# A merged last store, a new order of the later steps and another split of block products between engines in a polysketch-attention plus FFN kernel

## The chip, the cores and the metric

The kernel runs on one core of a Trainium2 chip. The metric is device time in microseconds of one execution. A core has five engines that run side by side, each with its own queue of instructions: TensorE (PE; its weight loads are shown as PEld), VectorE (DVE), ScalarE (ACT), GpSimd (POOL) and SyncE (SP, which here issues nearly all DMA transfers; ScalarE issues a few). They meet through semaphores: an instruction waits until the one that it depends on has told that it is done.

## The reference: what is computed

Two blocks, one after the other. q, k and v come in float32, the sketches and the weights in float64 (loaded as 64-bit words and turned into float32 by integer steps); the result is float32.

```
a_x = x @ S1.T;  b_x = x @ S2.T                      # x = q or k, 4 batches, 4 heads, 1088 rows, 32 wide; 8 sketches
phi(x) = outer(a_x, b_x), 64 values a row
kv = phi(k).T @ v ;  z = sum of phi(k) over the rows
attn = (phi(q) @ kv) / (phi(q) @ z + 1e-6)            # (4, 4, 1088, 32)
x = attn as (4352, 128)                               # 4352 = 4 batches x 1088 tokens, heads side by side
out = ((x @ w1) * (x @ w2)) @ w3 @ w_out              # w1, w2: 128 x 1024, w3: 1024 x 1024, w_out: 1024 x 128
```

## The kernel before, in words

The program is not written as loops in the order of execution. `make_steps` defines some 1100 named steps, each a function that issues a few instructions, and the string `ORDER` (lines 63 to 127) lists all names in the order in which they are issued. The launcher at the end runs them one by one and chains the instructions of each engine in that order, so the order of the string is the order of every engine's queue. `POOL` (line 51) is the set of steps that go to GpSimd rather than VectorE; `on(name)` looks them up. `SLOTS` (line 28) gives, string by string, the buffer that each new tile of a kind takes: `b` the eight PSUM banks, `m` 32 SBUF buffers, and so on; one character per tile, in the order in which the steps ask for them. A tile that takes a buffer must wait until the readers of its former tile are through.

The work in stages:

- Steps `k0` to `k3` load keys and values of a batch, make phi(k) and the small matrices `kq` that stand for kv and z; steps `w0` to `w10` turn the 64-bit weight words into float32 (`w*.load`, `.c`, `.m` on ScalarE, `.j` on VectorE, `.a0`, `.a1` on POOL), and `f0` to `f7` fold w3 with w_out into `w3o`, so that the FFN's last two products are one.
- Steps `q0` to `q3` make the attention output of batches 0 and 1, half a batch each (512 tokens). `g0` to `g3` are their FFN: per chunk c of 128 of the 1024 columns `g0.0a` and `g0.0b` (products with w1 and w2, lines 1655 and 1665), `g0.0c` (copy of the first to SBUF, ScalarE, 1660), `g0.0m` (product of both, VectorE, 1671), `g0.0o` (product with w3o, line 1690).
- `q4` and `q6` are batches 2 and 3, 1024 tokens at once. Each goes through `tr`, `max`, `l2`, `l1`, `rm`, the sketch products on PE (`A0`, `C0`, `C1`, 32-row tiles that use four PSUM banks), their transposes on VectorE (`At`, `Ct`), splits (`sm`, `st`, `sh`, `sl`, `sc`), products and sums (`al`, `p01`, `p2`, `p12`, `dn`, `de`, `rc`), scaling of the outputs by powers of two (`bs`, `na`, `nb`, `nm`, `nr`, `ne`, `nn`), then `phi0`, `phi1`, their transposes `pT0`, `pT1` (VectorE), the product with kq (`x`, PE, line 1477) and four copies out of the banks, `xT0` and `xT2` on ScalarE, `xT1` and `xT3` on VectorE. `q4.ns` and `q6.ns` (POOL, lines 1444 and 1447) square the scales and spread them over the partitions, one small product and 16 small copies each; only the steps `oS` read the result. `qr` is the same chain for the last 64 tokens of each of the four batches.
- `h4` and `h6` replace the first two products of the FFN for the tokens of q4 and q6 (each of them 1024 tokens, the g4/g5 and g6/g7 of the third product). The products with w1 and w2 are done by blocks, with seven block products in place of eight (`prod`, line 1602): names such as `h4.1b6` are batch part h4, column block 1 (of 4), side b, product 6. Side a (w1) uses rows 0 to 63 of the array, side b (w2) rows 64 to 127. Products 1, 6, 7 and 4 add up in one PSUM tile X, 5 and 3 in Y, 2 stands alone in Z; between them ScalarE copies the sum so far to SBUF (`take`, line 1609: c, d, e, i) and VectorE adds a PSUM tile to such a copy (`plus`, line 1614: f, g, h). The sums of moving data that products 3, 5, 6 and 7 need are `h4.s1` to `h4.s4`; those of the weights are `v.1` to `v.4` (POOL). The elementwise product of sides a and b is `h4.1m11`, `m12`, `m22` (line 1636, VectorE or POOL by the set) and `m21` (line 1641, VectorE). The third product is then `g4.0o` to `g7.7o` (line 1690).
- A result leaves by `oT` (transpose out of PSUM, VectorE, line 1697), for g4 to g7 `oS` (product with the scales, line 1703), and `st`: four DMAs of 64 KB issued by SP (`main_dst`, line 1506).
- `gr` is the FFN of the 256 tokens of qr: `gr.0a`, `gr.0b`, `gr.0c`, `gr.0m` with 256 columns, and `gr.0o0`, `gr.0o1` for the two halves of 128 tokens (line 1679). `gr.oT0` (ScalarE) and `gr.oT1` (VectorE) copy the halves out of PSUM (line 1714); `gr.st0` is issued by ScalarE and `gr.st1` by SP, 64 KB each (`rest_dst`, line 1512).

Before the third product of g4 to g7 PE goes through the h4 and h6 products in four stretches: 18 products up to `qr.x`, 38 up to the g5 products, 14 between the g5 and the g4 products, 42 up to the first `gr` product.

At 34 us, in a part of the order that the diff leaves alone, PE runs `g0.6b`, `g0.0a`, `k1.T0`, `k1.T1`, and ScalarE `k2.max` (reads the keys of batch 2 as they land), `g0.7c`, `g0.4c`, `k1.Gc`, `g0.0c`.

The functions that the diff touches, and what calls them:

Of the kernel before, what the change touches and what calls it, by code (L numbers as in the profile page):

```python
# [43 lines left out]

# [4 lines left out]
QUARTERS = (0, 2, 1, 3)  # L49

POOL = set("""
    g5.oS g7.oS h4.0m12 h4.0m22 h4.1m11 h4.1m12 h4.1m22 h4.2m12 h4.2m22 h4.s4 h6.0m11 h6.0m12 h6.1m11
    h6.1m12 h6.1m22 h6.2m22 h6.3m11 h6.3m22 h6.s2 h6.s3 k0.Nh k0.Nr k0.rest0 k1.Nr k1.kp0 k1.kp1
    k1.rest0 k2.Nr k2.rest0 k3.kp0 k3.kp1 k3.rest0 q0.al q0.p01 q0.sca q1.al q1.p12 q1.phi q2.bs q2.p01
    q2.p2 q2.phi0 q2.sc q3.al q3.bs q3.p12 q3.p2 q3.phi0 q4.al q4.bs q4.nn q4.p12 q4.phi0 q4.phi1 q4.sc
    q6.al q6.p01 q6.p12 q6.p2 q6.phi1 q6.sc q6.sl qr.al qr.bs qr.p12 qr.p2 qr.phi0 qr.sl s.AR s.KS s.Pp
    s.blkh s.low
""".split())

# [31 lines left out]
g2.4b g2.2b g2.6b k3.Ta g2.3b k3.Tb k3.Tc q4.l1 g2.7m g2.4m q3.phi0 q3.pT0 w3.c kr1.kp g2.0m g2.3m g2.6m g2.2m w2.a1  # L91
w2.a0 q3.x w6.a0 f4.m w3.j f6.t w3.a1 q3.xT0 g3.4a w8.c f4.o g3.4c g3.1a q4.rm q4.A0 k3.ab q4.C0 q4.C1 k3.N0 k3.N1
k3.abt g3.3b g3.7b w3.a0 q4.At q4.Ct g3.6a f6.m g3.7a g3.0a q4.sm f0.t w4.c f6.o w6.a1 k2.kp1 f3.t g3.1c g3.6c k3.kp1
g3.0c f0.m g3.4b f3.m f3.o k3.kp0 k2.kp0 k2.kv0 k2.kv3 k2.kv1 k2.kv2 w4.j k2.kvr k2.kvc q4.st q4.sh q4.sl q4.sc k3.kv0
k3.kv1 w10.load q4.al k3.kv3 k3.kv2 k3.kvr w4.m g3.7c k3.Na f0.o k3.Nb w8.m g3.4m q4.p01 q4.p2 q4.p12 g3.0b g3.6b
w5.a0 g3.6m q4.dn g3.0m g3.2b q4.de g3.2a g2.0o v.s w8.j q4.rc g3.7m v.t w8.a1 w4.a1 g3.2c w8.a0 g2.4o k3.kvc w10.c
w10.m g3.0o g2.6o g3.3a g3.3c g3.4o f2.t q4.na w4.a0 q6.tr q6.max g3.1b g3.3m f5.t g3.1m f2.m k3.Nr q6.l2 q6.l1 f5.m
f5.o f2.o g3.5a f1.t q4.bs g3.5c q6.rm q6.A0 q6.C0 q6.C1 g2.5o q4.nb q4.nm q4.nr q4.ne q6.Ct q6.At k2.kqt g3.3o f1.m
g3.5b q6.sm q4.nn q4.phi0 q4.phi1 g3.2m q4.pT0 w10.j w10.a0 q4.pT1 g1.0o w10.a1 g3.5m q6.st q6.sh f7.t qr.rm k2.kq
# [33 lines left out]
def make_steps(ctx, tc, q, k, v, S1, S2, moe_w1, moe_w2, moe_w3, moe_w_out, out):  # L133
# [11 lines left out]
    NT = S // 32  # L145
# [1362 lines left out]
                             oT[i * 32:(i + 1) * 32, :nT * 32].rearrange("p (T d) -> p T d", d=32))  # L1508
        return dst

    def rest_dst(oT, u):
        (sp if u else act).dma_start(bass.AP(tensor=out.tensor, offset=(NT - 2 + u) * DM,
                             ap=[[NT * DM, 32], [S * DM, B], [1, DM]]), oT)
# [129 lines left out]
    def ffn(g, n, dst, halves=1):  # L1643
# [38 lines left out]
        if g != "r":  # L1682
            first = {}
            turn = [c for i in range(4) for c in (i, i + 4)] if whole else range(NC)
            for c in range(NC):
                @step(f"g{g}.{c}o")
                def _(c=c):
                    if c == turn[0]:
                        o_ps[g] = ps("out", [128, 512], "ps_o")
                    pe.matmul(o_ps[g], w3o[:, c], ab_sb[g, c], start=c == turn[0], stop=c == turn[-1])  # L1690

            oT = {}

            @step(f"g{g}.oT")
            def _():
                oT[0] = sb("oT", [128, 512], bufs=2)
                dve.transpose(oT[0], o_ps[g])

            if whole:
                @step(f"g{g}.oS")  # L1700
                def _():
                    y = oT[0].rearrange("p (t d) -> p t d", d=32)
                    on(f"g{g}.oS").tensor_mul(y, y, bview(scale[g], [[1, 16], [0, 32]]))

            step(f"g{g}.st")(lambda: dst(oT[0]))
        else:
            z = {}
            for u in range(2):
                @step(f"g{g}.oT{u}")
                def _(u=u):  # L1710
                    if u == 0:
                        z["o"] = sb("oT", [128, 512], bufs=2)
                    z[u] = z["o"][:, u * DM:(u + 1) * DM]
                    (dve.tensor_copy if u else act.copy)(z[u], o_ps[g, u])
# [76 lines left out]
```

## Time and profile before

| | |
|---|---|
| runs | 254.11, 254.26 and 259.58 us; median 254.26 |
| the profiled execution | 253.4 us, of which 251.3 us lie between its first and last instruction (the span) |
| granted TensorE clock, mean | 0.996 |
| PE busy, first to last quarter of the first 100 us | 23.78, 23.85, 24.99 and 25.00 of 25 us each |
| DMA | 22.06 MB, 88 GB/s over the span |

All times of a trace are counted from the start of the span; an execution takes some 2 us more than its span. A row of the timeline gives start, duration, engine, line, operation, what it writes and reads, how many instructions are merged in it, and in brackets how long the engine had been idle before and what ended that. A `q` behind an engine's name (SPq) means its sequencer, which waits or issues DMAs. The views of waits say who waited for what: total, number, longest.

Most of PE's float32 matmuls are recorded as two passes of one instruction each. The end of a matmul is modelled, so its starts tell more than its busy time.

### The profile page before, as it was taken

What the parts mean: (1) busy time and instruction counts of PE and PEld (TensorE: products, weight loads), DVE (VectorE), ACT (ScalarE), POOL (GpSimd) and SP (SyncE); (2) the same over time, 40 slices, a digit from 0 to 9 for tenths busy, and PEclk for the clock granted to TensorE, in tenths of its full rate; (3) what the DMA queues carried; (4) which work ended last, traced back from release to release, by engine and by line L of the source; (5) the groups of instructions that cost most, each with busy time, mean ns of one, the idle gap of its engine ahead of it and who ended that gap; (6) DMA issues with size and microseconds to landing.
All of it is one profiled execution on the core that took longest, in us unless ns stands there. A gap on an engine that the chain in (4) does not pass through costs nothing.

```text
span 251.3 us, 6572 instructions
## 1 busy us (share of the span) xinstructions
PE 242.8 (97%) x2678; PEld 139.0 (55%) x2678; DVE 189.0 (75%) x385; ACT 123.6 (49%) x244; POOL 133.6 (53%) x181
## 2 busy tenths in 40 slices
PE   8999989999999999999999999998999999999991
PEld 5887545555554567847645544544555445645671
DVE  2798997999799989988898989847746347781540
ACT  2999946755787742397223006664424145521010
POOL 4533977356649786365759498589241322910100
PEclk9999999999999999999999999999999999999998
DMA  7596978486778965000000000540000000000441
GB/s 203 169 264 210 248 185 189 113 250 163 191 181 251 212 170 133 3 0 4 0 3 0 3 1 3 96 75 0 0 0 0 3 0 0 0 0 3 69 80 40
DMA packets 32078, 22.06 MB, mean 88 GB/s; under 512 B 21296, under 2 KB 26672, under 8 KB 32048
## 3 DMA queue, kind: packets, MB, share of 16 engines
q1 hardware_dynamic: 31360, 21.05, 34.0%
q10 hardware_dynamic: 688, 0.59, 0.7%
q8 instruction: 21, 0.34, 0.6%
q14 instruction: 9, 0.07, 0.1%
HBM read 19.40 MB, written 2.23 MB: 86 GB/s over the span
## 4 chain that ended last, share of the span: by engine, by line
PE 82%; DMA 7%; POOL 4%; ACT 2%; SPq 1%; issue 1%; DVE 1%; POOLq 0%; DVEq 0%
PE ps_o L1690 22%; PE b_ps L1665 12%; PE a_ps L1655 11%; PE ps_X L1602 9%; PE ps_w3o L484 6%; PE ps_Y L1602 4%; DMA k<-in_k_dram 3%; PE ps_Z L1602 3%; PE idle_ps L232 3%; POOL nz L1447 2%; PE ps_ac L1324 2%; DMA raw<-in_moe_w_dram 2%; PE ps_x L1477 2%; PE ps_kv L719 2%; DMA kr<-in_k_dram 2%; PE ps_g L609 1%
## 5 line engine op out<-in xcount | busy, mean ns | idle before, releaser
L1602 PE MATMUL ps_X<-xd,wv 64*128 64x512 f32 x112 | 41.1, 598 | 0.7 <-ACT hc L1609 0.7
L1660 ACT COPY ffa<-a_ps 128x512 f32<-128x512 f32 (+1 forms) x40 | 21.0, 544 | 31.5 <-PE a_ps L1655 31.2
L1655 PE MATMUL a_ps<-xT,w 128*128 128x512 f32 (+1 forms) x80 | 35.6, 557 | 0.4 <-DVE kabt L695 0.4
L1665 PE MATMUL b_ps<-xT,w 128*128 128x512 f32 (+1 forms) x80 | 35.9, 561 | 0.0
L1609 ACT COPY hc<-ps_X 128x512 f32<-128x512 f32 x40 | 22.3, 591 | 24.3 <-PE ps_X L1602 13.6
L1636 POOL TENSOR_TENSOR hc<-hc 128x512 f32<-128x512 f32 x15 | 20.0, 1360 | 24.9 <-DVE hc L1614 24.7
L1671 DVE TENSOR_TENSOR ab<-ffa,b_ps 128x512 f32<-128x512 f32 (+1 forms) x40 | 24.0, 619 | 9.2 <-ACT ffa L1660 4.6
L1690 PE MATMUL ps_o<-ab,w3o 128*128 128x512 f32 x64 | 29.2, 597 | 0.0
L1690 PE MATMUL ps_o<-hc,w3o 128*128 128x512 f32 x64 | 29.0, 595 | 0.0
L451 POOL TENSOR_TENSOR w3c<-w3c,cv_m 128x512 int32<-128x512 int32 x16 | 21.1, 1340 | 5.9 <-DVE w3c L445 5.9
L1602 PEld LDWEIGHTS ps_X<-xd,wv 64*128 64x128 f32 x112 | 17.1, 186 | 12.8 <-issue 6.3
L1655 PEld LDWEIGHTS a_ps<-xT,w 128*128 128x128 f32 x80 | 14.3, 190 | 14.0 <-issue 8.6
L1665 PEld LDWEIGHTS b_ps<-xT,w 128*128 128x128 f32 x80 | 14.2, 190 | 13.3 <-issue 9.0
L1602 PE MATMUL ps_Y<-xd,wv 64*128 64x512 f32 x48 | 20.9, 591 | 0.0
L1690 PEld LDWEIGHTS ps_o<-hc,w3o 128*128 128x128 f32 x64 | 12.0, 190 | 13.3 <-issue 11.2
L1690 PEld LDWEIGHTS ps_o<-ab,w3o 128*128 128x128 f32 x64 | 11.7, 190 | 13.7 <-issue 13.4
L1614 DVE TENSOR_TENSOR hc<-hc,ps_Y 128x512 f32<-128x512 f32 x16 | 10.8, 683 | 10.0 <-PE ps_Y L1602 9.2
L484 PEld LDWEIGHTS ps_w3o<-wo,w3T 128*128 128x128 f32 x128 | 15.2, 192 | 2.7 <-issue 2.4
L484 PE MATMUL ps_w3o<-wo,w3T 128*128 128x128 f32 x128 | 15.6, 276 | 0.0
L1614 DVE TENSOR_TENSOR hc<-hc,ps_Z 128x512 f32<-128x512 f32 x16 | 10.7, 680 | 6.3 <-PE ps_X L1602 5.1
L240 ACT ACTIVATE cv_c<-raw 128x1024 f32<-128x1024 f32 x11 | 13.0, 1182 | 3.6 <-DVE kabt L695 1.8
L1490 ACT COPY xd<-ps_x 64x256 f32<-64x256 f32 x16 | 5.9, 366 | 17.1 <-PE ps_x L1477 16.9
(315 smaller groups left out, 511.9 us busy)
## 6 DMA issues: line engine op xcount, KB each, us to landing
raw<-in_moe_w_dram SPq DMA_DIRECT2D x32, 256.0 KB, 4.9
qh<-in_q_dram SPq DMA_DIRECT2D x4, 544.0 KB, 3.8
out_dram<-oT SPq DMA_DIRECT2D x33, 64.0 KB, 1.9
raw<-in_moe_w_dram SPq DMA_DIRECT2D x4, 512.0 KB, 5.4
k<-in_k_dram SPq DMA_DIRECT2D x3, 512.0 KB, 7.5
v<-in_v_dram SPq DMA_DIRECT2D x2, 512.0 KB, 4.5
kh<-in_k_dram SPq DMA_DIRECT2D x8, 128.0 KB, 2.8
raw<-in_moe_w_out_dram SPq DMA_DIRECT2D x4, 256.0 KB, 5.1
```

The costliest lines, as they stand in the source:

```text
L240: act.activation(dst, hi.bitcast(F32), ACT.Prelu, scale=2.0 ** -112, alpha=-2.0 ** 32)
L451: pool.tensor_tensor(d, d, x["m"][:, i * 512:(i + 1) * 512], ALU.add)
L484: pe.matmul(t["o"], w3T[ko][:, c], wo[:, c], start=c == 0, stop=c == NC - 1)
L1602: pe.matmul(x[bank], stat(j, u)[:, i * 128:(i + 1) * 128], rows(j, u), start=new, stop=True, tile_position=(u * 64, 0), skip_group_check=True)
L1609: act.copy(x[k], x[bank])
L1614: dve.tensor_add(x[k], x[k], x[bank])
L1636: on(f"h{g}.{i}m{k}").tensor_mul(both[0][k], both[0][k], both[1][k])
L1655: pe.matmul(x["a"][:, :w], w_of(0, c), xT[g][:, c0:c0 + w], start=True, stop=True)
L1660: act.copy(x["s"][:, :w], x["a"][:, :w])
L1665: pe.matmul(x["b"][:, :w], w_of(1, c), xT[g][:, c0:c0 + w], start=True, stop=True)
L1671: dve.tensor_mul(ab_sb[g, c][:, c0:c0 + w], x["s"][:, :w], x["b"][:, :w])
L1690: pe.matmul(o_ps[g], w3o[:, c], ab_sb[g, c], start=c == turn[0], stop=c == turn[-1])
```

## The change

The diff does four things.

1. `gr.st0` and `gr.st1` become one step, `gr.st1`: one DMA of 128 KB by SP for both halves, behind both copies.
2. `ORDER` is the old one up to `q4.l1 g2.7m g2.4m q3.phi0 q3.pT0`, some 85 us into the span, and new behind that. `SLOTS` follows the new order; the string `b` differs from its 53rd character on, which is the tile of `g0.0a`.
3. The set `POOL` changes. To POOL: g4.oS, g6.oS, h4.0m11, h4.2m11, h4.3m11, h4.3m22, h4.s1, h4.s2, h4.s3, h6.2m11, h6.2m12, h6.s4, k2.kp0, k3.Nr, q4.sl, q6.nm, qr.p01. From POOL to VectorE: h4.0m12, h4.0m22, h4.1m12, h6.1m11, h6.1m22, h6.3m11, h6.3m22, h6.s3, k3.kp1, q4.nn, q4.p12, q6.al, q6.sl, qr.al, qr.p12.
4. In the new order `q4.ns` and `q6.ns` stand among the g4 products instead of among the h4 products; `g4.st` and `g5.st` stand before and in the h6 products instead of behind the g7 products; `qr.A0` to `qr.C1` come some eight PE steps later; and the products of h4 and h6 are permuted.

The core of the diff, with the places of the order that are spoken of below:

```diff
 SLOTS = {
     "b": 
-        "012345670475204615036021764164752756475430257310436025143625021423716041605374160537645276"
...
+        "012345670475204615036021764164752756475430257310436014253164062563721052104375210437154671"
...
-g0.0o g0.1o g0.2o g1.7o q6.na q6.rc q6.bs q6.nb q6.nm g2.2o g0.6o g0.3o g2.1o g3.7o qr.sl qr.sc q6.nr q6.ne q6.nn
-q6.phi0 qr.al q6.pT0 q6.phi1 q6.pT1 qr.p01 qr.p2 v.1 g2.7o g0.5o q6.x q6.xT2 g3.oT g1.oT q6.xT0 h4.s2 qr.p12 g0.4o
...
-qr.xT0 h4.0b4 h4.0m12 h4.0m21 h4.1a7 h4.2bc h4.1a5 h4.1ad h4.2b2 g3.st g2.st g1.st h4.2a5 h4.1b1 h4.2b6 h4.1bc q4.ns
-q6.ns h4.2a1 h4.2ac h4.1a3 h4.2bh h4.2b5 h4.1ag h4.2bd h4.1b6 h4.1a4 h4.0m22 h4.1af h4.1be h4.2a6 h4.2b3 h4.2be h4.1bf
...
-gr.0m h6.2m11 gr.6a gr.6c gr.2b g6.1o g6.5o gr.1b g4.oS gr.5m gr.1m gr.6m g6.2o g6.6o g6.3o g7.oS g7.st g6.7o gr.3b
-g5.st gr.0o0 gr.0o1 gr.3a gr.3c g4.st gr.6o1 gr.6o0 gr.5o0 gr.5o1 gr.1o0 gr.4o0 gr.7m g6.oT g6.oS g6.st gr.3m gr.3o0
-gr.1o1 gr.2c gr.2m gr.2o0 gr.4o1 gr.3o1 gr.7o0 gr.2o1 gr.oT0 gr.st0 gr.7o1 gr.oT1 gr.st1
...
+q6.p01 q6.p2 q6.p12 g3.6o q4.xT3 h4.s1 h4.s3 g0.5o f7.m f7.o g1.6o qr.A0 qr.C0 qr.C1 q6.dn g1.3o g1.4o g2.2o q6.de
+q6.rc q6.na q6.bs qr.At q6.nb g3.2o g3.5o qr.sm qr.Ct h4.s2 q6.nm q6.nr qr.st qr.sh qr.sl qr.sc g0.4o g1.5o g2.1o
+qr.al g1.2o g1.7o q6.ne q6.nn qr.p01 g3.7o q6.phi0 q6.pT0 q6.phi1 q6.pT1 qr.p2 v.1 v.2 q6.x g2.7o qr.p12 g0.7o q6.xT0
...
+g4.1o g4.5o g4.2o g4.6o g4.3o h6.0bf g4.7o h6.1bc q6.ns h6.1b2 h6.0ag h6.0a4 h6.1a6 h6.0a3 h6.0b7 q4.ns g4.oT h6.0bg
...
+h6.1a7 g4.oS h6.1ag g4.st h6.1a2 h6.1bf h6.1ah h6.1af g5.oS h6.2a6 h6.2bc h6.3b1 h6.1b7 h6.3b2 h6.1a4 h6.2ae h6.3bc
...
+g7.3o gr.0m g7.7o gr.3b gr.0o0 gr.0o1 gr.6o1 gr.5o1 g6.oT g6.oS g6.st g7.oT gr.1o1 gr.6o0 gr.5o0 gr.1o0 g7.oS gr.4m
+gr.4o1 gr.7m gr.3m gr.3o1 gr.4o0 gr.2o1 gr.7o1 g7.st gr.3o0 gr.2o0 gr.7o0 gr.oT0 gr.oT1 gr.st1
...
-    def rest_dst(oT, u):
-        (sp if u else act).dma_start(bass.AP(tensor=out.tensor, offset=(NT - 2 + u) * DM,
-                             ap=[[NT * DM, 32], [S * DM, B], [1, DM]]), oT)
+    def rest_dst(oT):
+        sp.dma_start(bass.AP(tensor=out.tensor, offset=(NT - 2) * DM,
+                             ap=[[NT * DM, 32], [S * DM, B], [1, 2 * DM]]), oT)
...
                     if u == 0:
                         z["o"] = sb("oT", [128, 512], bufs=2)
-                    z[u] = z["o"][:, u * DM:(u + 1) * DM]
-                    (dve.tensor_copy if u else act.copy)(z[u], o_ps[g, u])
-
-                step(f"g{g}.st{u}")(lambda u=u: dst(z[u], u))
+                    (dve.tensor_copy if u else act.copy)(z["o"][:, u * DM:(u + 1) * DM], o_ps[g, u])
+
+            step(f"g{g}.st1")(lambda: dst(z["o"][:, :2 * DM]))
```

More of the change, by code (lines that the diff above doesn't have):

```diff
@@ L51 @@
 POOL = set("""
[L52 to L56, printed above, removed]
+    g4.oS g5.oS g6.oS g7.oS h4.0m11 h4.1m11 h4.1m22 h4.2m11 h4.2m12 h4.2m22 h4.3m11 h4.3m22 h4.s1 h4.s2
+    h4.s3 h4.s4 h6.0m11 h6.0m12 h6.1m12 h6.2m11 h6.2m12 h6.2m22 h6.s2 h6.s4 k0.Nh k0.Nr k0.rest0 k1.Nr
+    k1.kp0 k1.kp1 k1.rest0 k2.Nr k2.kp0 k2.rest0 k3.Nr k3.kp0 k3.rest0 q0.al q0.p01 q0.sca q1.al q1.p12
+    q1.phi q2.bs q2.p01 q2.p2 q2.phi0 q2.sc q3.al q3.bs q3.p12 q3.p2 q3.phi0 q4.al q4.bs q4.phi0 q4.phi1
+    q4.sc q4.sl q6.nm q6.p01 q6.p12 q6.p2 q6.phi1 q6.sc qr.bs qr.p01 qr.p2 qr.phi0 qr.sl s.AR s.KS s.Pp
     s.blkh s.low
@@ L90 @@
 g2.0c w8.load w4.load v3.zero v3.loadr v2.load v3.load v2.loadr k2.Nr g0.2m g1.6m w7.a1 w7.a0 f4.t k3.T0 k3.T1 g2.0b
[L91 to L99, printed above, removed]
@@ L125 @@
-gr.1o1 gr.2c gr.2m gr.2o0 gr.4o1 gr.3o1 gr.7o0 gr.2o1 gr.oT0 gr.st0 gr.7o1 gr.oT1 gr.st1
+g2.4b g2.2b g2.6b k3.Ta g2.3b k3.Tb k3.Tc q4.l1 g2.7m g2.4m q3.phi0 q3.pT0 q3.x g2.2m g2.6m f6.t g2.0m q3.xT0 kr1.kp
+w6.a0 w2.a0 w2.a1 w6.a1 f4.m w3.c g3.7a f4.o g3.7c q4.rm w3.j g2.3m g3.0a f3.t w3.a0 w3.a1 w4.c g3.0c q4.A0 k3.ab
+k3.abt w5.a0 q4.C0 q4.C1 k3.N0 q4.At k3.N1 k3.Na g3.7b f6.m q4.Ct k3.kp0 g3.7m q4.sm f0.t g3.1a g3.1c g3.6a g3.6c w8.c
+k3.kp1 q4.st k2.kp1 k3.Nb g3.1b f3.m g3.3b g3.4b g3.4a k2.kp0 f0.m w10.load g3.3a f0.o k3.kv0 g3.4c w8.m q4.sh qr.rm
@@ new lines @@
+f2.t k2.kv0 k2.kv3 k2.kv1 k2.kv2 k3.kv1 k3.kv3 k3.kv2 k2.kvr g3.1m g3.4m k3.kvr w10.m f6.o w10.c w4.m k3.kvc k2.kvc
+g3.0b q4.sl q4.sc q4.p01 q4.al w4.j q4.p2 g3.0m w8.j q4.p12 w4.a1 w4.a0 g2.0o g2.4o q6.tr q4.dn q4.de q4.rc f2.m
+k2.kqt v.s f3.o k3.kqt k3.kq g3.3c g1.0o g3.6b g3.5a q6.max g3.5c f2.o q6.l2 f1.t g3.2a g3.2c g3.3m w8.a1 k3.Nr w8.a0
+f1.m g2.6o g3.2b k2.kq f1.o q6.l1 q4.bs g3.6m w10.j f5.t q4.na q4.nb q4.nm q6.rm g3.2m q4.nr g3.0o f5.m f5.o q6.A0
+q6.C0 q6.C1 q4.ne q4.nn w10.a1 q4.phi0 g3.4o q4.phi1 q6.Ct g3.5b g2.5o g3.3o g3.1o v.t q6.At q4.pT0 q4.pT1 w10.a0
@@ new lines @@
+h4.0bc h4.0a5 h4.0ah g0.oT h4.s4 h4.0ae h4.0bd h4.0b6 h4.1b5 h4.0bh h4.0a7 h4.0be h4.0ad h4.0ag qr.phi0 qr.pT0 v.4
+h4.1a1 h4.0b3 h4.2b1 h4.0a3 h4.0a4 h4.0b7 h4.1bd h4.1ac h4.0ai h4.0bf h4.0af h4.1a6 h4.1b3 h4.1ae qr.x qr.xT0 h4.0bg
+h4.2bc h4.0b4 h4.1a7 h4.0m21 h4.2b2 h4.1a5 h4.2a1 h4.1b1 h4.2bh g0.st h4.2a2 h4.1ad h4.1bc h4.1ag h4.0m12 h4.2b6
+h4.1b6 h4.1a3 h4.2ac h4.1a4 h4.2b5 h4.2ah h4.1af h4.1be h4.0m22 h4.2bd h4.1ai g2.st g3.st h4.2a5 h4.1b7 h4.1bf h4.1m12
+h4.2ad h4.3b1 h4.2a6 h4.2ae h4.2be h4.3b5 h4.2b3 h4.3a1 h4.3ac h4.1bg h4.1m22 h4.2a3 h4.2b7 h4.2a7 h4.2af h4.2ag
@@ new lines @@
+h4.3bc h4.3a6 h4.2bg h4.2bf h4.3bd h4.3b6 h4.1b4 h4.3a5 h4.3be h4.2m22 h4.1m21 h4.3ae h4.3b3 h4.2a4 h6.0a1 h4.3b7
+h4.3bf h4.2m12 h4.3ad h4.3a7 h4.1b2 h4.1a2 h4.3bg h4.3ag h4.3m22 h4.2ai h4.2b4 h4.3a3 h4.3b2 h4.2m21 h4.3b4 h4.3a4
+g5.0o g5.4o g5.1o g5.5o h4.3ai h4.3m21 h4.3af h6.s1 gr.0a gr.0c h6.0ac h4.2m11 h6.s3 h6.s2 h4.3bh h4.1ah g5.2o g5.6o
+g5.3o gr.4a g5.7o g5.oT h4.0m11 gr.4c h4.3m12 h6.s4 h4.3a2 h6.0b1 h6.0b5 h4.3ah h4.1bh h4.1m11 h6.0a6 h6.0bc h6.0a5
+h6.1a5 h6.0b2 h6.1a1 h6.0b6 h6.0bd h6.0ad h6.0ae h6.0b3 h6.1ad h6.1ac h6.0be h6.0bh h6.1b1 h6.0a7 g4.0o g4.4o h4.3m11
```

44 lines of the change are left out of this document (17 added, 27 removed).

## The prediction

> **What bounds the kernel now.** I read the page's busy times, then a table by stretches, then the waits and the timeline of each engine around every place where TensorE (PE) stands still.
>
> ```profile
> PE 242.8 (97%) x2678; PEld 139.0 (55%) x2678; DVE 189.0 (75%) x385; ACT 123.6 (49%) x244; POOL 133.6 (53%) x181
> ```
>
> PE bounds the kernel. The change leaves every matmul as it is, so only three things can move: time in which PE stands or runs half full, and what lies behind its last matmul. Half full needs a look at the block products (L1602): each uses 64 of the 128 rows, a on the lower half, b on the upper.
>
> ```profile
> 174.61 0.69 PE L1602 MATMUL ps_X<-xd,wv 64*128 64x512 f32 x1 [0.71 <-ACT hc L1609]
> 174.62 0.69 PE L1602 MATMUL ps_Y<-xd,wv 64*128 64x512 f32 x1
> 175.14 0.59 PE L1602 MATMUL ps_X<-xd,wv 64*128 64x512 f32 x1
> 175.15 0.59 PE L1602 MATMUL ps_Y<-xd,wv 64*128 64x512 f32 x1
> 175.57 0.59 PE L1602 MATMUL ps_Z<-xd,w 64*128 64x512 f32 x1
> ```
>
> From 174.61 on two passes start side by side every 0.43 us: the halves run at once. A product is two passes, 0.85 us. The 112 products (224 passes) are 56 pairs: 56 x 0.853 = 47.8 us if always paired. They stand in four stretches:
>
> ```profile
> 154.20:162.60 8.40, 8.32 (x36) 1.00 0.36 62
> 163.30:181.80 18.50, 17.76 (x76) 1.00 0.15 26
> 189.70:196.10 6.40, 6.38 (x28) 1.00 0.00 0
> 203.00:222.30 19.30, 19.21 (x84) 1.00 0.00 0
> ```
>
> (Columns: window, its length, PE busy, passes, clock.) Together 52.6 us, 52.2 without the windows' rims. Going in costs some 0.1 us each time (the first pass takes 0.53 instead of 0.43 above) and so does going out: 0.8 for four. 52.2 - 47.8 - 0.8 = 3.6 us are lost, though busy reads nearly full. The second stretch has 19 pairs: 16.2 + 0.2 against 18.4, a loss of 2.0; the other three lose 1.6. Elsewhere from 50 us on PE is dense.
>
> **The change part by part.** *One store for two.* Rows of the end (SP's queue, ScalarE's, VectorE's, SP's longest wait):
>
> ```profile
> 242.94 5.17 SPq L1506 DMA_DIRECT2D out_dram<-oT  x4
> 248.20 0.62 SPq L1512 DMA_DIRECT2D out_dram<-oT  x1
> ```
>
> ```profile
> 245.46 0.27 ACT L1714 COPY oT<-ps_or 128x128 f32<-128x128 f32 x1 [2.03 <-PE ps_or L1679]
> 245.75 0.65 ACTq L1512 DMA_DIRECT2D out_dram<-oT  x1
> ```
>
> ```profile
> 245.90 0.29 DVE L1714 COPY oT<-ps_or 128x128 f32<-128x128 f32 x1 [1.97 <-PE ps_or L1679]
> ```
>
> ```profile
> SPq L1506 <- DMA out_dram<-oT: 3.4, 1, 3.4
> ```
>
> PE ends at 245.87, the last copy at 246.19, yet the last store is issued at 248.20. SP's four stores of g6 take 5.17 us because the fourth waits 3.4 us for a DMA to land: it shares a landing counter (the program has eight, given in turn over both queues) with ScalarE's store of 245.75, and starts when that has landed, two microseconds later. With ScalarE's store gone the last four-piece store and the merged one wait only for counters of pieces issued long before. Then the merged store starts at PE's end + 0.03 + 0.27 (ScalarE copies last now) + 0.03, if SP is free. SP has g6.st and g7.st ahead of it (rows for eight issues, a transpose, a scaling on POOL, the small products):
>
> ```profile
> 234.31 4.14 SPq L1506 DMA_DIRECT2D out_dram<-oT  x8
> ```
>
> ```profile
> 241.47 0.72 DVE L1697 STREAM_TRANSPOSE oT<-ps_o 128x512 f32<-128x512 f32 x1 [2.28 <-PE ps_o L1690]
> ```
>
> ```profile
> 233.23 1.05 POOL L1703 TENSOR_TENSOR oT<-oT,nz 128x512 f32<-128x512 f32 x1 [12.20 <-DVE oT L1697]
> ```
>
> ```profile
> 242.58 3.29 PE L1679 MATMUL ps_or<-w3o,ab 128*128 128x128 f32 x28
> ```
>
> Eight issues take 4.14 us, four 2.1. In the new order g7.7o is followed by one 256-column product (0.43) and 16 small ones (28 passes in 3.29, so 32 in 3.7): it ends 4.1 before PE. Transpose 0.72, scaling on POOL 1.05, hand-overs 0.15, issues 2.1: SP is free 0.1 before PE's end; g6.st, two g7 products earlier, is through by then. So 2.33 us behind PE's end become 0.33: -2.0. The store is twice as big; price by the page's DMA rows:
>
> ```profile
> raw<-in_moe_w_dram SPq DMA_DIRECT2D x32, 256.0 KB, 4.9
> ...
> raw<-in_moe_w_dram SPq DMA_DIRECT2D x4, 512.0 KB, 5.4
> ```
>
> 0.5 us for 256 KB more, 0.13 for 64 KB. Tail: -1.9 (ends -1.2, if g7's scaling comes 1 us late, and -2.0). g4.st and g5.st move to the middle; their eight issues lie beside PE there. The buffers that they free are wanted again by copies of h6.3 some 5 us after they land: no cost.
>
> *The scales q4.ns and q6.ns move behind the h4 products on POOL.* Now they stand among them (POOL's timeline, then ScalarE's):
>
> ```profile
> 163.93 3.54 POOL L1447 COPY nz<-nz 32x8 f32<-32x8 f32 x16
> ...
> 171.43 4.96 POOL L1636 TENSOR_TENSOR hc<-hc 128x512 f32<-128x512 f32 x4
> ```
>
> ```profile
> 172.74 0.59 ACT L1609 COPY hc<-ps_X 128x512 f32<-128x512 f32 x1 [1.42 <-POOL hc L1636]
> 173.97 0.59 ACT L1609 COPY hc<-ps_X 128x512 f32<-128x512 f32 x1 [0.65 <-POOL hc L1636]
> ```
>
> The two blocks (16 copies each, a product ahead of each) hold POOL from 163.7 to 171.4; h4.0m22 and h4.1m12 stand behind them, ScalarE's copies wait for the buffers of these (1.42 and 0.65), and PE for the copy (the 0.71 before 174.61; one half had run dry before that). In the new order 0m22 and 1m12 are VectorE's, and POOL has only 1m22, 2m22 and 2m12 there, each done 1 to 2.5 us before PE wants what the copy behind it gives, by slots of 0.853. The block is the bulk of this stretch's 2.0; I take -2.0 (ends -0.7, the visible gap alone, and -2.05). Their 7.7 us now run beside the g4 products, ahead of g4.oS only.
>
> *The new order of the block products.* Pairs, stretches (9, 19, 6, 22) and passages are as many as before. A product that waits for a copy of its own chain needs a distance of two on its half (0.43 + 0.59 for the two passes, 0.04, the copy's 0.59, 0.04: 1.69 of 1.71 us); both orders keep at least two, and distances of exactly two are five in each. Of the other 1.6 us I take -0.7, between all of it (-1.6) and a new wait like the one removed (+0.9).
>
> *Which engine.* POOL had 15 of the block products, now 14; but h4.s1 to s3 and h6.s4 come to it, and h6.s3 goes:
>
> ```profile
> L1636 POOL TENSOR_TENSOR hc<-hc x15: 1265/1276/1737, 162.4 to 219.8; 128x512 f32<-128x512 f32 x15
> L1636 DVE TENSOR_TENSOR hc<-hc x9: 682/692/1342, 159.9 to 235.4; 128x512 f32<-128x512 f32 x9
> ```
>
> 1.28 us on POOL for 0.69 on VectorE. PE covers both engines there; uncovered, each piece moved costs 0.6.
>
> *A bank earlier than the new order.* The string of PSUM banks differs already at g0.0a, where the order is still the old one: it takes the bank of g0.7a, which g0.7c must first have read; k1.T0 takes that of g0.4a. ScalarE's and PE's timelines there:
>
> ```profile
> 34.34 1.16 ACT L184 ACTIVATE k_abs<-k 128x1152 bf16<-128x1152 f32 x1 [3.08 <-DMA k<-in_k_dram]
> ...
> 35.50 1.05 ACT L1660 COPY ffa<-a_ps 128x512 f32<-128x512 f32 x2
> ```
>
> ```profile
> 34.83 1.10 PE L1655 MATMUL a_ps<-xT,w 128*128 128x512 f32 x2 [0.40 <-DVE kabt L695]
> ...
> 36.69 0.25 PE L840 MATMUL ps_T<-RS,G_c 128*32 128x32 f32 x2 [0.52 <-ACT G_c L820]
> ```
>
> ScalarE waits 3.08 us for k's load; g0.7c and g0.4c are the two copies behind it, the first through at 36.06, the second at 36.55. g0.0a, started at 34.83, must wait to 36.1: 1.27 late. PE then no longer waits the 0.52 for G_c, so +0.75 remains (ends 0 and +1.27), and as PE is dense from there it reaches the end.
>
> *The stretch from 85 to 154 us, reordered.* Adding up VectorE's and POOL's work queued ahead of each PE step, in the old order's durations, leaves 0.5 us or more everywhere, in the new order as in the old; the swaps between the two engines (k2.kp0 to POOL and k3.kp1 from it, nine small steps of q4, q6 and qr) are in that sum. One chain is tighter (POOL's q6.phi1, VectorE's q6.pT1, PE's q6.x):
>
> ```profile
> 144.35 2.99 POOL L1459 TENSOR_TENSOR ph<-s_al,s_bs 128x1024 f32<-128x1024 f32 x1 [0.78 <-DVE s_bs L1440]
> ```
>
> ```profile
> 147.38 1.25 DVE L1467 STREAM_TRANSPOSE pT<-ph 128x1024 f32<-128x1024 f32 x1 [0.57 <-POOL ph L1459]
> ```
>
> ```profile
> 150.94 1.50 PE L1477 MATMUL ps_x<-pT,kq 32*32 32x256 f32 x64
> ```
>
> q6.x comes 2.3 us after its last transpose now. In the new order qr.At stands in VectorE's queue ahead of q6.nb and q6.phi0 and waits for qr.C1 on PE, which moves 3.7 us later, and POOL's three h4 sums (3.8 us) come ahead of q6.nm. With these durations: qr.C1 is through at 142.3 (3.7 later than now, and the 0.75), VectorE then has 4.0 to 4.9 us of queue up to q6.nn, POOL 2.99 for q6.phi1, VectorE 1.25: 150.6 to 151.5. PE is at q6.x at 151.8, 0.3 to 1.2 later. I take +0.4 for this stretch (ends 0 and +1.5).
>
> Sum: -1.9 - 2.0 - 0.7 + 0.75 + 0.4 = -3.45 us. The profiled execution took 253.4 (span 251.3), 0.9 under the median of 254.26; against its own time that is 249.95 (span 247.85), against the median 250.8.
>
> **The rivals.** *The h4 wait comes back behind another.* VectorE, with 0m12, 0m22 and 1m12, hands buffers late, or v.4 (POOL, due within 0.2 us of h4.0a4) holds the first stretch. For it: VectorE makes every PSUM sum of these stages. Against, all engines in the second stretch (PE, weight loads, VectorE, ScalarE, POOL):
>
> ```profile
> 163.30:181.80 18.50, 17.79 (x86) 9.19 (x77) 12.38 (x20) 9.84 (x21) 12.87 (x40) 1.00 0.15 26
> ```
>
> VectorE is busy 12.4 of 18.5 us, and the changed m products give and take as much. In this rival only the tail, the bank and the 0.4 remain: -0.75, 253.5.
>
> *q6.x becomes the stop, and the kernel slower.* If the chain slides by all of 3.7 + 3.8 us, against 2.3 of slack, PE stands 5.2 us at q6.x: 250.8 + 5.2 = 256.0. It makes the kernel slower from a slide of 2.3 + 3.45 = 5.8 us on. Against: the three sums can run while VectorE still works on q6's sums of products, as the sum above has it.
>
> *Strict order on PE.* If the halves had to start in program order, a neighbour on the same half would cost 0.43 more. There are 33 such neighbours now (75 alternations, 4 exits) and 37 then: +1.7 in place of the -2.7 above: 255.2. But strict order would make 75 x 0.427 + 37 x 0.853 = 63.6 us of the old stretches, and they took 52.2; hence the low chance. [...]
>
> *The merged store brings nothing,* because SP is still busy with g7.st or the bigger store lands 2 us later: 252.7.
>
> **How the numbers follow.** Forecast 0.62, the wait come back 0.17, q6.x 0.12, strict order 0.03, store without gain 0.06. Tail, scales and order at their good ends and no new wait, with the bank as worked out, give -2.0 - 2.05 - 1.6 + 0.75 = -4.9, so 249.4, a little less if k's load lands earlier; the range 249.0 to 254.2 takes in the first and the last rival and leaves out most of the two slow ones. The forecast's own range is 249.3 to 252.5. 2% is 5.1 us, about what a measurement of this kernel tells from no change: under 249.2 is faster, over 259.3 slower. Faster 0.06, same 0.91, slower 0.03.
>
> **What would show it.** Right: no SP wait of 3 us on a landing; the merged store issued within 0.6 us of PE's end; PE idle about 1.3 us more near 35 and 0.5 less at G_c; the 19-pair stretch in 16.4 to 17 us, no ScalarE wait on POOL there; q6.x directly behind its neighbours. Wrong: a gap at q6.x or h4.0a4, a first copy of h4 or h6 waiting for POOL, VectorE late with buffers, or the last store queued behind g7's.

## The result, and the profile after

The changed kernel took 251.81 us (median of all its executions), the kernel before 254.19 on the same occasion: a ratio of 0.990, with an interval of 0.986 to 0.993. A second measurement gave 251.85 against 254.00, 0.9925 (0.988 to 0.997). So it is faster by 0.75 to 1%, some 2 us. Some executions of each kernel show a lower granted clock (of the changed kernel one of 256.26 us at 0.986, beside three of 250.94 to 251.97 at 1.00) and take 1 to 2% longer: the ratios, the intervals and all medians from the second measurement on leave them out, and of the profile with the scales moved back, which fell on such an execution both times, only a stretch at a granted clock of 1.00 is read.

The profiled execution took 251.97 us, its span 250.2 (before: 253.4 and 251.3). The two traces differ by less than the medians, 1.1 us of span; what follows explains these 1.1, and 0.35 us outside the span.

PE's work is the same, as forecast:

```profile
PE 242.1 (97%) x2678; PEld 138.9 (56%) x2678; DVE 188.0 (75%) x383; ACT 123.0 (49%) x244; POOL 133.9 (54%) x183
```

**The end of the kernel.** SP's queue, then PE's last products (timeline of the kernel after):

```profile
242.09 4.46 SPq L1506 DMA_DIRECT2D out_dram<-oT  x8
247.02 0.62 SPq L1512 DMA_DIRECT2D out_dram<-oT  x1
```

```profile
242.96 3.73 PE L1679 MATMUL ps_or<-w3o,ab 128*128 128x128 f32 x32
```

The eight stores follow each other without a wait of 3 us, and the last is issued at 247.02. PE ends at 242.96 + 3.73 = 246.69: 0.33 us between them, where it was 2.33.

A little more is gained outside the span, that is, in an execution's time less its span. This is 2.07 to 2.20 us in every execution of the two programs in which ScalarE issues the first of the last two stores (the kernel before, and the one experiment below that moves only the scales), and 1.74 to 1.85 us in every execution of the eight programs in which SP issues all of them, whether one or two. So with the store on ScalarE's queue some 0.35 us more was measured there too; why is open.

But PE itself ends 0.82 later than before (245.87). The rest of the section looks for that.

**The bank at 34 us.** ScalarE, then PE:

```profile
34.44 1.16 ACT L184 ACTIVATE k_abs<-k 128x1152 bf16<-128x1152 f32 x1 [3.18 <-DMA k<-in_k_dram]
...
35.60 1.05 ACT L1660 COPY ffa<-a_ps 128x512 f32<-128x512 f32 x2
```

```profile
36.31 1.10 PE L1655 MATMUL a_ps<-xT,w 128*128 128x512 f32 x2 [1.87 <-ACT ffa L1660]
```

g0.0a now starts, at 36.31, when ScalarE has read its bank. The gap is 1.87 in place of 0.40, and the 0.52 at G_c is gone: +0.95.

**From there to the block products.** q6.x (the view of its tile) and its last transposes:

```profile
L1477 PE MATMUL ps_x<-pT,kq x64: 373/374/403, 152.0 to 153.1; 32*32 32x256 f32 x64
```

```profile
L1467 DVE STREAM_TRANSPOSE pT<-ph x2: 1246/1246/1246, 147.9 to 149.7; 128x1024 f32<-128x1024 f32 x2
```

The second transpose ends at about 149.7 + 1.25 = 150.95, some 1.0 us ahead of q6.x, which waits for nothing. The block products start at 155.33 in place of 154.28: 1.05 later, of which the bank explains 0.95.

**The block products.** The table by stretches:

```profile
155.30:163.80 8.50, 8.45 (x36) 1.00 0.29 48
164.40:181.90 17.50, 17.41 (x76) 1.00 0.11 19
189.70:195.30 5.60, 5.50 (x24) 1.00 0.00 0
202.30:223.10 20.80, 20.32 (x88) 1.00 0.16 25
```

Without the windows' rims (from the first pass to the start of the next other matmul) the stretches take 8.38, 17.38, 5.46 and 20.75 us; before it was 8.27, 18.45, 6.31 and 19.16. A pair costs 0.853, and the third stretch has one fewer, the fourth one more. By stretch the loss changed by +0.11, -1.07, 0 and +0.73. So the second was shortened by half of what was forecast, and the fourth gave two thirds of that back.

The whole: bank +0.95, up to the block products +0.10, stretches -0.23, PE's end to the last issue -2.0, and from there to the end of the span +0.11 (3.06 before, 3.17 now, with a store twice as big; 0.13 was forecast): -1.1.

Where the halves of PE stand still now shows in two places. In the second stretch, ScalarE's copies, and POOL's first product of the stretch:

```profile
171.94 1.07 ACT L1609 COPY hc<-ps_X 128x512 f32<-128x512 f32 x2 [0.23 <-PE ps_X L1602]
173.69 1.07 ACT L1609 COPY hc<-ps_X 128x512 f32<-128x512 f32 x2 [0.67 <-PE ps_Y L1602]
```

```profile
172.67 1.27 POOL L1636 TENSOR_TENSOR hc<-hc 128x512 f32<-128x512 f32 x1 [12.26 <-DVE hc L1614]
```

POOL stands idle for 12.26 us, and ScalarE no longer waits for it. The two copies from 173.69 on are h4.3ac and h4.3bc. The second one's product was done at 171.9, but the first, ahead of it in ScalarE's queue, waits for PE. h4.3b6 needs the second, which ends at 174.76, and its half of the array loses 0.51 us. (Which half a pass belongs to is worked out from the order of the products and the tile names.)

In the fourth stretch, VectorE, PE and PE's weight loads:

```profile
205.25 0.69 DVE L1614 TENSOR_TENSOR hc<-hc,ps_X 128x512 f32<-128x512 f32 x1 [2.03 <-PE ps_Y L1602]
205.85 0.68 DVE L1614 TENSOR_TENSOR hc<-hc,ps_Z 128x512 f32<-128x512 f32 x1
...
209.51 0.69 DVE L1614 TENSOR_TENSOR hc<-hc,ps_X 128x512 f32<-128x512 f32 x1 [0.97 <-PE ps_X L1602]
210.12 0.68 DVE L1614 TENSOR_TENSOR hc<-hc,ps_Y 128x512 f32<-128x512 f32 x1
```

```profile
206.59 0.69 PE L1602 MATMUL ps_X<-xd,w 64*128 64x512 f32 x1 [0.45 <-DVE hc L1614]
```

```profile
210.85 0.18 PEld L1602 LDWEIGHTS ps_Z<-xd,w 64*128 64x128 f32 x1 [0.53 <-DVE hc L1614]
210.86 0.29 PEld L1602 LDWEIGHTS ps_X<-xd,wv 64*128 64x128 f32 x2
```

The first pair of VectorE rows is h6.0bg and h6.1bh. h6.1bh, which reads Z, could have run in the 2.03 us of idle time, but stands behind h6.0bg. It frees the bank that h6.2a1 writes; that starts at 206.59, 0.06 us after h6.1bh's end (205.85 + 0.68), and both halves have stood. At 210.85 h6.3b2 waits for the bank that the row of 210.12 reads, until 210.80. h6.1a4 is for the other half and its input (the row of 209.51) was ready at 210.20, yet its weights come only behind those of h6.3b2.

### The profile page after: what moved, and what is told of

It reads as the page before. It is cut to its first block, busy times and chain, and to the rows that moved or that the text cites. A ratio compares the mean times of both kernels' runs of the same rounds, so it can differ in the third digit from the quotient of the medians.

```text
span 250.2 us, 6598 instructions
## 1 busy us (share of the span) xinstructions
PE 242.1 (97%) x2678; PEld 138.9 (56%) x2678; DVE 188.0 (75%) x383; ACT 123.0 (49%) x244; POOL 133.9 (54%) x183
## 4 chain that ended last, share of the span: by engine, by line
PE 85%; DMA 8%; ACT 2%; SPq 2%; DVE 1%; issue 0%; ACTq 0%
PE ps_o L1690 22%; PE b_ps L1665 12%; PE ps_X L1602 12%; PE a_ps L1655 11%; PE ps_w3o L484 6%; PE ps_Y L1602 5%; DMA k<-in_k_dram 5%; PE ps_Z L1602 3%; PE ps_x L1477 2%; PE ps_ac L1324 2%; DMA raw<-in_moe_w_dram 2%; DMA kr<-in_k_dram 2%; PE ps_kv L719 2%; PE ps_g L609 1%; PE ps_or L1679 1%; ACT k_abs L184 1%
## 5 line engine op out<-in xcount | busy, mean ns | idle before, releaser
L1602 PE MATMUL ps_X<-xd,wv 64*128 64x512 f32 x112 | 42.4, 602 | 0.0
L1609 ACT COPY hc<-ps_X 128x512 f32<-128x512 f32 x40 | 22.9, 591 | 26.4 <-PE ps_X L1602 16.3
L1636 POOL TENSOR_TENSOR hc<-hc 128x512 f32<-128x512 f32 x14 | 17.5, 1270 | 34.2 <-DVE hc L1614 34.2
L451 POOL TENSOR_TENSOR w3c<-w3c,cv_m 128x512 int32<-128x512 int32 x16 | 20.4, 1289 | 7.5 <-DVE w3c L445 4.2
L1697 DVE STREAM_TRANSPOSE oT<-ps_o 128x512 f32<-128x512 f32 x8 | 5.7, 715 | 13.1 <-PE ps_o L1690 13.1
L1614 DVE TENSOR_TENSOR hc<-hc,ps_X 128x512 f32<-128x512 f32 x16 | 10.7, 684 | 6.1 <-PE ps_X L1602 3.4
L1459 POOL TENSOR_TENSOR ph<-s_al,s_bs 128x1024 f32<-128x1024 f32 (+1 forms) x6 | 11.8, 1981 | 4.5 <-DVE s_bs L1440 4.4
```

The lines of the kernel that those rows point to most:

```text
L451: pool.tensor_tensor(d, d, x["m"][:, i * 512:(i + 1) * 512], ALU.add)
L1459: on(nm(f"phi{u}")).tensor_mul(x, bview(s["al"][:, u * g], [[r, g], [1, r], [0, r]]), bview(s["bs"][:, u * g], [[r, g], [0, r], [1, r]]))
L1602: pe.matmul(x[bank], stat(j, u)[:, i * 128:(i + 1) * 128], rows(j, u), start=new, stop=True, tile_position=(u * 64, 0), skip_group_check=True)
L1609: act.copy(x[k], x[bank])
L1614: dve.tensor_add(x[k], x[k], x[bank])
L1636: on(f"h{g}.{i}m{k}").tensor_mul(both[0][k], both[0][k], both[1][k])
```

## The experiments

The theory after the result (theory 1 below): four causes at four places, the store's landing counter, the bank, the scales on POOL, and neighbours in a queue that hold each other up.

**The merged store alone** (`m1_store_only`), in the kernel before:

```diff
-gr.oT0 gr.st0 gr.7o1 gr.oT1 gr.st1
+gr.oT0 gr.7o1 gr.oT1 gr.st1
-    def rest_dst(oT, u):
-        (sp if u else act).dma_start(...
+    def rest_dst(oT):
+        sp.dma_start(...
```

> The kernel before with the merged store alone. Theory 1 (SP's fourth g6 store waited 3.4 us on the landing counter of ScalarE's store): that wait is gone, PE still ends at 245.9, and the one store is issued 0.35 us behind it in place of 2.33. Time 252.3 against 254.2, ratio 0.992. Rival a (only the saved issue of 0.62 us counts): 253.6, ratio 0.998. Rival b (the landing of the last bytes sets the end anyway): 254.2, ratio 1.000.

**Two stores, both by SP** (`m2_two_on_sp`), in the kernel before:

```diff
-        (sp if u else act).dma_start(bass.AP(tensor=out.tensor, offset=(NT - 2 + u) * DM,
+        sp.dma_start(bass.AP(tensor=out.tensor, offset=(NT - 2 + u) * DM,
```

> The kernel before with its two last stores kept apart, both issued by SP. Theory 1 (the cost lay in a landing counter that a store on another queue held): no SP wait of 3 us on a landing, the first store issued at about 245.8, the second 0.65 us later at about 246.4: 1.75 us less than before, 252.45, ratio 0.993, and 0.1 to 0.3 us behind the merged store. Rival (merging itself is what pays, or SP waits for the landing of its own earlier stores): 253.6 to 254.2, ratio 0.998 to 1.000, with the wait still there.

Measured: 0.992 (0.989 to 0.995) for the one, 0.9925 (0.989 to 0.996) for the other, medians 251.88 and 252.21 against 253.73. SP's and PE's last rows, of the merged store and then of the two stores:

```profile
238.64 7.48 SPq L1506 DMA_DIRECT2D out_dram<-oT  x10
247.50 0.62 SPq L1512 DMA_DIRECT2D out_dram<-oT  x1
```

```profile
244.26 2.84 PE L1679 MATMUL ps_or<-w3o,ab 128*128 128x128 f32 x24
```

```profile
239.00 6.92 SPq L1506 DMA_DIRECT2D out_dram<-oT  x9
246.79 1.29 SPq L1512 DMA_DIRECT2D out_dram<-oT  x2
```

```profile
244.29 2.62 PE L1679 MATMUL ps_or<-w3o,ab 128*128 128x128 f32 x22
```

With one store the issue is 0.40 us behind PE's end (247.10). With two by SP the first goes out before PE ends (246.91) and the second, at 247.50, 0.59 behind that end. In neither does SP wait for a store to land before it issues the last one (its waits there are 1.3 us for VectorE's copy and 0.8 for ScalarE's). Both gain the same. The traces name the counter too: before, ScalarE's store of 245.75 and SP's fourth store of g6 count on the same one (104), and the fourth store is issued only at 247.79, when that has counted (the last time at 247.77); in the changed kernel the fourth store has another (101) and is issued at 246.04, 0.04 us behind the third. With both last stores on SP it is issued at 245.43. So not the merging pays, but that no store on ScalarE's queue holds a landing counter that SP's earlier store needs. The rivals (one issue saved, no gain) fall.

One expectation failed: PE ends over 1 us later than the 245.87 of before in both traces, in an order that is the same up to there. ScalarE began on the keys of batch 2 at 35.50 and 34.71 in place of 34.34, which explains the delay of the first trace and a part of that of the second.

**The old bank** (`m3_after_banks`), in the changed kernel: in the string `b`, 1 and 2 are exchanged from the 53rd character to the end, and 4 and 5 too. Its start there:

```diff
...
-7310436014253164062563721052104375210437154671
+7310436025143265061463712041205374120537245672
...
```

> The changed kernel with its PSUM banks renamed from the 53rd character of the string on (1 and 2 exchanged, 4 and 5 exchanged), so that g0.0a takes the bank that it had before; order, engines and all later relations between banks as they are. Theory 1 (g0.0a waits for g0.7c's read of its bank): the gap of 1.87 us near 34.4 falls to 0.40, the 0.52 at G_c is back, PE ends 0.95 earlier; 250.85 against 251.8 for the changed kernel, ratio to before 0.987. Rival (the delay at 35 us is absorbed by later waits for loads): PE ends where it did, 251.8, ratio 0.990.

PE's timeline in it:

```profile
35.02 1.10 PE L1655 MATMUL a_ps<-xT,w 128*128 128x512 f32 x2 [0.38 <-DVE kabt L695]
36.59 0.25 PE L840 MATMUL ps_T<-RS,G_c 128*32 128x32 f32 x2 [0.23 <-ACT G_c L820]
```

The gaps are 0.61 together in place of 1.87, the stretches are those of the changed kernel to 0.01 us, and PE ends at 245.86 in place of 246.69, 0.83 earlier where 0.95 was expected: theory 1 in the trace. The times do not resolve it: 251.26, ratio 0.991 (0.987 to 0.995), beside 0.990 and 0.9925 for the changed kernel. The gap went with the load here: it was 1.25 in the second profile of the changed kernel, where ScalarE began on k 0.6 us earlier (33.83).

**Four neighbours exchanged** (`m4_after_queues`), in the changed kernel:

```diff
-h4.3a1 h4.3ac h4.1bg
+h4.3a1 h4.3bc h4.3ac h4.1bg
...
-h6.0bg h6.1b5 h6.1bh
+h6.1bh h6.0bg h6.1b5
...
-h6.3b2 h6.1a4
+h6.1a4 h6.3b2
...
-h6.0ah h6.1ai h6.2a5 h6.3bh
+h6.3bh h6.0ah h6.1ai h6.2a5
```

> The changed kernel with four neighbours in its order exchanged: h4.3bc ahead of h4.3ac (ScalarE), h6.1bh ahead of h6.0bg and h6.3bh ahead of h6.0ah (VectorE), h6.1a4 ahead of h6.3b2 (PE). Theory 1 (what the block products still lose is waiting in line behind a neighbour that isn't ready): the 19-pair stretch falls from 17.38 to about 16.9, the 22-pair stretch from 20.75 to about 19.5, 1.7 us in all: 250.1 against 251.8 for the changed kernel, ratio to before 0.984. Rival (another producer is late next, so that the waits only move): 0.4 us or less, 251.4, ratio 0.989.

Measured: 249.86 against 253.73, 0.985 (0.981 to 0.989). Its table by stretches (the second and the fourth) and VectorE:

```profile
164.40:181.50 17.10, 17.02 (x76) 1.00 0.11 18
...
201.80:221.80 20.00, 19.92 (x88) 1.00 0.16 26
```

```profile
203.11 0.69 DVE L1614 TENSOR_TENSOR hc<-hc,ps_Z 128x512 f32<-128x512 f32 x1 [0.34 <-PE ps_X L1602]
204.80 0.69 DVE L1614 TENSOR_TENSOR hc<-hc,ps_X 128x512 f32<-128x512 f32 x1 [1.01 <-PE ps_Y L1602]
```

h6.1bh now runs ahead of h6.0bg, in time that was idle. The second stretch fell from 17.38 to 16.95, the fourth from 20.75 to 19.88: 1.3 us, where theory 1 said 1.7 and the rival 0.4. The waits in line were the cause of most of what the new order lost; the three exchanges in the fourth stretch were not tried one by one.

**The scales alone** (`m5_before_ns`), in the kernel before:

```diff
-h4.1bc q4.ns
-q6.ns h4.2a1
+h4.1bc
+h4.2a1
...
-h4.1m11 h6.0b5
+h4.1m11 q6.ns q4.ns h6.0b5
```

> The kernel before with one edit: q4.ns and q6.ns stand behind h4.1m11, after POOL's last product of the h4 stage, in place of in the middle of it. Theory 1 (the two blocks held POOL's h4.0m22, 1m12 and 1m22, and these the copies that PE waited for): the 0.7 us gap of PE near 174 and ScalarE's waits for POOL are gone, the 19-pair stretch takes about 17.1 in place of 18.45, 1.3 us less: 252.65 against 253.95, ratio 0.995. Rival (the products on POOL are late on their own, as they take 1.27 us there against 0.69 on VectorE): the stretch stays above 18.1, ratio 0.999 to 1.000.

Measured: 251.65 against 253.68, 0.992 (0.988 to 0.996). Its 19-pair stretch:

```profile
163.90:180.90 17.00, 16.92 (x76) 1.00 0.17 28
```

16.88 us from pass to pass, 1.57 less than before (1.3 expected), with h4.0m22 and 1m12 still on POOL. The gap near 174 is gone. The rival (POOL too slow for these products) falls. This one move did more for the stretch than the whole change (17.38).

**The scales back in the changed kernel** (`m6_after_ns_back`, and again as `n2_after_ns_back` beside the changed kernel):

```diff
-h4.1ad h4.1bc h4.1ag
+h4.1ad h4.1bc q4.ns q6.ns h4.1ag
...
-h6.1bc q6.ns h6.1b2
+h6.1bc h6.1b2
-h6.0b7 q4.ns g4.oT
+h6.0b7 g4.oT
```

> The changed kernel with q4.ns and q6.ns back at their old place, behind h4.1bc among the h4 products. Theory 1 (moving the blocks away was not needed: with h4.0m12, 0m22 and 1m12 on VectorE, POOL stands idle from 160.4 to 172.7, and the blocks' 7.7 us end at about 168, ahead of h4.1m22's inputs at 172.5): the 19-pair stretch stays at 17.4, all else too, 251.8, ratio to before 0.991. Theory 2 (the blocks' place is what counts): POOL is late again, the stretch goes back to 18.2 or more, 252.7, ratio 0.995.

> The changed kernel with the scales back among the h4 products, beside it on the same chip. Theory 1 (their place doesn't matter once VectorE has three of the products): the 19-pair stretch 17.4, time within 0.3 us of the changed kernel. Theory 2 (it does): 0.9 us or more above it, a ratio to before higher by 0.0035.

Measured: 0.9965 (0.994 to 0.999) the first time, 0.991 (0.9875 to 0.995) the second, beside 0.9925 for the changed kernel on the same chip. The first agreed with theory 2, the second, which has the direct comparison, with theory 1. The traces decide: in both the stretch takes 17.38 us. POOL's timeline and the stretch in the second:

```profile
163.60 3.54 POOL L1447 COPY nz<-nz 32x8 f32<-32x8 f32 x16
167.22 0.20 POOL L1444 TENSOR_TENSOR nz<-nz 128x8 f32<-128x8 f32 x1
167.48 4.10 POOL L1447 COPY nz<-nz 32x8 f32<-32x8 f32 x16
175.50 1.27 POOL L1636 TENSOR_TENSOR hc<-hc 128x512 f32<-128x512 f32 x1 [3.92 <-DVE hc L1614]
```

```profile
167.30:184.70 17.40, 17.38 (x76) 1.00 0.11 20
```

The blocks end at 171.6, POOL then stands idle for 3.92 us, and the stretch takes 17.38 as in the changed kernel. So there the move of the scales is worth nothing: POOL is already free, as three of its products are on VectorE. Moving the scales takes the wait away without those products on VectorE, and the changed kernel has no such wait without the move. That the products on VectorE would do it alone, in the old order, was not tried. Why the first measurement was 0.5% slower stays open.

**The changed kernel again, both repairs, and the old kernel with two edits** (`n1_after`; `m7_best` and again `n3_after_repairs`, the bank and the four exchanges together; `m8_before_store_ns` and again `n4_before_two_edits`, the kernel before with the merged store and the scales moved, nothing else). n1 to n4 ran on one chip.

> The changed kernel again, unaltered, on one chip with the next three. Theory 1 (the sum of its parts by the traces: store -1.95, h4 stretch -1.07, h6 stretch +0.73, bank +0.95, all else +0.2): 1.1 us under before, 252.8 against 253.9, ratio 0.9955; the first measurement of 0.990 was then helped by loads that landed early in its three runs. Rival (something in it gains time that the two profiles happen not to show): 251.4, ratio 0.990.

> The changed kernel with both repairs: banks renamed so that g0.0a takes its old one, and the four exchanged neighbours. Theory 1 (both act at different places and add up): gap near 34.4 of 0.4, stretches of 16.95 and 19.88, PE ends 0.8 earlier than with the exchanges alone; 249.3, ratio to before 0.9815. Rival (what is won at 35 us is lost at the next wait for a load or at q3.x near 86 us, where PE stood 0.45 when the exchanges alone came early): 250.2, ratio 0.985.

> The changed kernel with old bank for g0.0a and the four exchanges, beside it on the same chip. Theory 1 (bank -1.0, exchanges -1.3): 2.3 us under the changed kernel, ratio to before 0.9865. Rival (the bank's microsecond is lost again at the loads): 1.3 us under it, ratio 0.9905.

> The kernel before, its old order, banks and engines, with two small edits: the merged store and the scales moved behind h4.1m11. Theory 1 (the tail and the one wait in the h4 stage are all that there was to win; the rest of the new order brings nothing): 1.95 and 1.3 add up to 3.25 us less, 250.7, ratio 0.987, that is 1 us under the changed kernel. Rival (the new order is worth its own time): 251.8 or more, ratio 0.992 or above.

> The kernel before with the merged store and the scales moved, beside the changed kernel on the same chip. Theory 1 (the rest of the change costs more than it brings): tail -1.95, h4 stretch -1.55, 3.5 us under before, ratio 0.986, 2.4 under the changed kernel. Rival (the new order is worth its own time): at or above the changed kernel.

| kernel | median us | ratio to before | interval |
|---|---|---|---|
| changed (`n1_after`) | 251.85 | 0.9925 | 0.988 to 0.997 |
| changed, both repairs (`m7_best`) | 250.39 | 0.988 | 0.986 to 0.991 |
| the same (`n3_after_repairs`) | 249.59 | 0.984 | 0.979 to 0.989 |
| before, two edits (`m8_before_store_ns`) | 250.51 | 0.990 | 0.986 to 0.994 |
| the same (`n4_before_two_edits`) | 250.95 | 0.987 | 0.982 to 0.993 |

The changed kernel with both repairs is the fastest of the ten programs by its second measurement, 2.3 us under the changed kernel there, as theory 1 had it. Its first is no better than the exchanges alone (0.985), as that rival had it, so the times don't prove the bank's share. The kernel before with two small edits is 0.9 us under the changed one on the same chip, where theory 1 said 2.4, and level with it by the ratios of the two first measurements (0.990); the intervals overlap. That the rest of the new order costs time is so by the traces (block products lose 2.84 us with the two edits, 4.19 in the changed kernel), and likely but not shown by the times. The changed kernel's second ratio lies between the sum of the traces (0.9955) and the first measurement.

## Why the prediction was right or wrong, point by point

The time lay in the range, 1.0 us above the forecast value; the sign was right, and so was that it stays under 2%. The sum was not: -3.45 forecast, -1.1 in the traces. That the time came nearer to the forecast than the sum is luck: what the measured difference has beyond the 1.1 was in no term of the sum (last paragraph of this section).

- *One store for two*, -1.9: right. 2.33 us behind PE's end became 0.33, and the two experiments on the store show the counter as cause. The 0.35 us outside the span were not foreseen. The rival that it brings nothing falls.
- *The scales move away*, -2.0: right as a cause, too large here. Alone it brings 1.57. In the changed kernel the stretch gained 1.07, and with the scales moved back it is as short, so that the move is not needed for it. The forecast took nearly the whole loss as won, as if no other wait stood behind this one; one did, h4.3bc behind h4.3ac, and the stretch took 17.38 us where 16.4 to 17 was named as the sign of being right.
- *The new order of the block products*, -0.7: wrong, also in its sign. The first, third and fourth stretch lost 0.84 more, close to the bad end that was named (+0.9). The step that failed is the test that every product keeps "a distance of two" from the copy that it waits for. It looks at one chain. The copies and sums of all chains stand in one queue on each engine, and a product also waits for a bank that a sum of another chain must free first: h6.1bh, ready early, came late behind a neighbour, with 2.03 us of idle time ahead of both, and held the bank of h6.2a1 until 206.53. The four exchanges gave back 1.3 us. (The stretches are not "as many as before" either: by the prediction's own table, 28 and 84 passes, the last two had 7 and 21 pairs, and now have 6 and 22. The sum does not change by it.)
- *A bank earlier than the new order*, +0.75: right, +0.95 in this trace.
- *85 to 154 us*, +0.4: +0.1, and q6.x had some 1.0 us of slack where 0.3 to 1.2 were forecast.
- *Which engine*: costed at nothing, as "PE covers both engines there". By POOL's timeline with the scales moved back it is what keeps POOL free in the h4 stretch of the changed kernel, with or without their move.
- The rivals: the h4 wait did not come back on POOL, but a smaller one on ScalarE and VectorE took part of its place. q6.x did not stop PE. Strict order on PE falls once more. These are the passes about 212 us (the X rows are h6.2b6, the Y row is h6.2a5, which is ahead of h6.2b6 in the program):

```profile
212.06 0.69 PE L1602 MATMUL ps_X<-xd,wv 64*128 64x512 f32 x1
...
212.59 0.59 PE L1602 MATMUL ps_X<-xd,wv 64*128 64x512 f32 x1
212.68 0.59 PE L1602 MATMUL ps_Y<-xd,wv 64*128 64x512 f32 x1
```

h6.2b6 starts at 212.06, 0.62 us ahead of h6.2a5 (212.68), which stands before it and is for the other half of the rows.

The measured difference, 2 to 2.4 us, is larger than the 1.1 of the traces. Of the rest 0.35 lies outside the span. The execution profiled before was 0.8 us under the median of its runs and the one profiled after 0.2 above its own. Why executions of one program differ by that much was not traced; that the time at which loads land is a part of it is the author's estimate, from ScalarE's start on the keys, 34.44 in one profile of the changed kernel and 33.83 in the other.

## What to carry to other kernels

When an order of steps changes, check each engine's queue and not only each chain: here a short operation that was ready early (h6.1bh) stood behind one that wasn't, and the 2.03 us of idle time beside it didn't help. Two cures for one wait did not add up here (the scales moved brought the stretch 1.57 us alone, and nothing in the changed kernel); take the wait away in a second kernel by each alone before both are counted. SP's queue was held for 3.4 us by a store on ScalarE's queue that shared a counter with one of its own, so the last stores of this kernel are better issued by one engine (251.88 and 252.21 us against 253.73).

## What the runs showed of the hardware that was not expected

- The loads of the first 35 us landed at other times in each profile, though all programs here have the same order up to there, and the spread, 1.8 us, is as large as most terms here. ScalarE's start on the same keys, first in the kernel before with the scales moved, then in that with the merged store, the earliest and the latest of the twelve profiles other than those of the scales moved back:

```profile
33.69 1.16 ACT L184 ACTIVATE k_abs<-k 128x1152 bf16<-128x1152 f32 x1 [1.80 <-DMA k<-in_k_dram]
```

```profile
35.50 1.16 ACT L184 ACTIVATE k_abs<-k 128x1152 bf16<-128x1152 f32 x1 [3.16 <-DMA k<-in_k_dram]
```

- About 212 us a product of one half of PE's rows started 0.62 us ahead of an earlier one of the other half (above), but at 210.85 the other half's next product did not pass: its input was ready at 210.20, a product of the first half stood before it and waited for VectorE until 210.80, and its weights came at 210.86, some 0.6 us late.
- With a last store on ScalarE's queue an execution also took some 0.35 us more outside the span (2.07 to 2.20 in place of 1.74 to 1.85), as said of the end of the kernel.
